# A state-space scan in chunks of 128 tokens with larger array tiles, ahead of routed experts

## The chip, the cores and the metric

The kernel runs on one core of one Trainium2 chip. The core has a matrix engine, TensorE (PE in the rows, with its weight loads as PEld), VectorE (DVE), ScalarE (ACT), GpSimd (POOL) and SyncE (SP, used here to issue DMAs). The metric is the device time of one execution in microseconds (us). All data are 32-bit floats except where the routing uses small whole numbers in bf16. In a profile's rows a 32-bit product appears as two weight loads and two matmuls (MATMUL, MM below); a transpose by the identity appears as one of each.

## The reference

Two stages. The first is a gated linear scan for 4 batches of 8 heads, 768 tokens, head size 32 and state size 16:

```python
for c in range(nc):                        # chunk = 32 tokens
    cum = np.cumsum(log_a[chunk], axis=-1)
    M = (Cc @ Bc.T) * exp(cum_i - cum_j) * causal
    y[chunk] = M @ xc + (Cc @ state) * exp(cum)
    state = exp(cum[-1]) * state + sum_j(Bc_j * xc_j * exp(cum[-1] - cum_j))
```

The size of the chunk is free: any one gives the same y. The second stage takes the 3072 tokens, 256 wide (8 heads side by side), finds for each the expert (of 8) with the largest cosine, and computes

```python
out[mask] = gate_w[mask, None] * (np.maximum(x[mask] @ w1[e], 0.0) @ w2[e])   # 256 -> 1024 -> 256
```

## The kernel before, in words

**Units.** A unit is 128 tokens of one batch, so there are 24, taken in pairs p = 0 to 11; chunk c (128 tokens of all 4 batches) holds the pairs 2c and 2c+1. Decays are divided out beforehand: `scale_b` scales B by the inverse decay (DVE), `scale_c` spreads the decay over partitions with a product by a 0/1 matrix (L251) and multiplies C by it (`cp`, DVE). The 8 heads of a unit lie in four groups q of 32 partitions, two heads (v = 0, 1) to a group with 16 states each.

**The products of a pair.** The scan itself runs in half chunks of 64 tokens (h = 0, 1), on small tiles of the PE array. `inner` (L312): 32 products of B and C, one for each head and half, on tiles of 32 rows by 64 columns, 64 columns moving. `outputs` (L340): 32 products of the carried state with C, on tiles of 32 by 32; and (L351) 32 products of the masked B-C products `g` with x, on tiles of 64 by 32. `sums` (L266): 16 products of B and x that give a chunk's contribution to the state. `finish` (L371): 4 products that turn the output back into rows of tokens and add the logits. `turn_b` (L233): 2 transposes. L251: 2 products. Together 120 products and transposes. `split_b` makes two copies of B, each with the other head of a group set to zero by `tmask` (ACT). `states` carries the state from half chunk to half chunk (DVE) and leaves it in `T`.

**The order.** `mamba` is a software pipeline: turn i of its loop does `inner` of pair i, `outputs` of pair i-1, `finish` of pair i-2, and the preparations of pair i+2. PE runs this in the order in which it is written (`manual_schedule`); the other engines' queues are ordered by a scheduler. In every odd turn from 5 on, `place` (L532) finds with bf16 products where the tokens of an earlier chunk go, and POOL sends them to the experts' lists in DRAM by four indirect DMAs (L546); `pick` prepares that on DVE. `load` and `load_weights` issue the DMAs of inputs and experts' weights from SP.

**After the scan** (`moe`), the experts' lists are read back (`xg`), transposed, and run through two layers of 128x128 products with 416 tokens moving (L635, L649), expert by expert. The change does not touch this part.

PSUM has 8 banks: `pg` takes four, `py` two, `pz` two.

Of the kernel before, what the change touches and what calls it, by code (L numbers as in the profile page):

```python
# [46 lines left out]
def build_consts(k):  # L47
# [15 lines left out]
    nc.vector.memset(k.heads[:, 0:Q:SQ], 1.0)  # L63
# [7 lines left out]
    k.mask = k.mc.tile([128, HQ], F32, name="mask")  # L71
    nc.gpsimd.memset(k.mask[:], 1.0)
    for h in range(2):
        m = k.mask[HQ * h : HQ * h + HQ]
        nc.gpsimd.affine_select(
            out=m, in_=m, pattern=[[1, HQ]], compare_op=ALU.is_ge, fill=0.0, base=0, channel_multiplier=-1
        )
# [23 lines left out]
def decays(k, kk):  # L101

    nc = k.nc
    tt = nc.vector.tensor_tensor
    a, f, r = k.a0[:, kk, :], k.f[:, kk, :], k.r[:, kk, :]
    clip(k, a)
    at = k.mc.tile([128, 4], F32, name=f"at{kk}")
    nc.vector.tensor_copy(out=at[:], in_=a[:, 0:Q:SQ])
    nc.vector.memset(a[:, 0:Q:SQ], 0.0)
    nc.vector.tensor_tensor_scan(out=f, data0=a, data1=k.heads[:], initial=0.0, op0=ALU.mult, op1=ALU.add)  # L110
    w = k.mc.tile([128, 2, 2], F32, name=f"w{kk}")
    tt(out=w[:, 0, :], in0=f[:, SQ - 1 : Q : HQ], in1=at[:, 1:4:2], op=ALU.mult)
# [15 lines left out]
def between(k):  # L128

    nc = k.nc  # L130
    a = k.a1
    clip(k, a[:])
    at = k.mc.tile([NB * NH, NK], F32, name="at")
    nc.vector.tensor_copy(out=at[:], in_=a[:, SQ:S:HQ])
    nc.vector.memset(a[:, SQ:S:HQ], 0.0)
    one = k.mc.tile([NB * NH, S], F32, name="one")
    nc.vector.memset(one[:], 0.0)
    nc.vector.memset(one[:, SQ:S:HQ], 1.0)
    p = k.mc.tile([NB * NH, S], F32, name="p")
    nc.vector.tensor_tensor_scan(out=p[:], data0=a[:], data1=one[:], initial=0.0, op0=ALU.mult, op1=ALU.add)  # L140
    k.g = k.mc.tile([NB * NH, NK - 1], F32, name="g")
    nc.vector.tensor_tensor(out=k.g[:], in0=p[:, HQ + SQ - 1 : S : HQ], in1=at[:, 1:], op=ALU.mult)


def spread_between(k):

    nc = k.nc
    ps = k.pz[:, 1, 448 : 448 + NB * (NK - 1)]
    for b in range(NB):
        nc.tensor.matmul(  # L150
            ps[:, (NK - 1) * b : (NK - 1) * (b + 1)], lhsT=k.spread[0:32, b, :], rhs=k.g[:], start=True, stop=True
        )
    k.whole = k.mc.tile([128, NK - 1, NB, 2], F32, name="whole")
    for v in range(2):
        nc.vector.tensor_scalar(
            out=k.whole[:, :, :, v], in0=ps.rearrange("p (b k) -> p k b", b=NB), scalar1=k.tmask[:, v : v + 1],
            scalar2=None, op0=ALU.mult,
        )
# [31 lines left out]
def load(k, c):  # L190
# [7 lines left out]
    t.st = k.inp.tile([128, 2, NB, 64], F32, name="st", tag="st", bufs=2)  # L198
# [37 lines left out]
def split_b(k, p):  # L236

    s = k.un[p] = Net()
    s.bt = k.work.tile([128, 2, 2, Q], F32, name="bt", tag="bt", bufs=3)
    for v in range(2):  # L240
        k.nc.scalar.activation(s.bt[:, v], k.pz[:, :, 264:392], ACT.Copy, scale=k.tmask[:, v : v + 1])


def scale_c(k, p):
# [5 lines left out]
    for i in range(2):  # L250
        nc.tensor.matmul(  # L251
            k.py[:, i, 384:512], lhsT=k.spread[g : g + 32, b + i, :], rhs=k.f[g : g + 32, c // 4, :],
            start=True, stop=True, tile_position=(g, 0),
        )
    s.cp = k.work.tile([128, 2, Q], F32, name="cp", tag="cp", bufs=4)
    nc.vector.tensor_tensor(out=s.cp[:], in0=t.ct[:, b : b + 2, :], in1=k.py[:, :, 384:512], op=ALU.mult)


def sums(k, p):

    c, b, t = pair(k, p)
# [12 lines left out]
def keep_sums(k, p):
    c, b, t = pair(k, p)
    k.nc.scalar.copy(  # L276
        out=t.st[:, :, b : b + 2, :], in_=k.py[:, :, 256:384].rearrange("p h (b m) -> p h b m", b=2)
    )


def states(k, c):


    nc = k.nc
    st = k.ld[c].st
    for h in range(2):
        i = 2 * c + h
        if i > 0:
            k.T[i] = k.stp.tile([128, NB, 2, D], F32, name="T", tag="T", bufs=6)
            nc.vector.tensor_tensor(  # L290
                out=k.T[i][:], in0=k.V[:].rearrange("p b (t d) -> p b t d", t=2),
                in1=k.whole[:, i - 1].unsqueeze(3).to_broadcast([128, NB, 2, D]), op=ALU.mult,
            )
        if i == 0:
            nc.vector.tensor_copy(out=k.V[:], in_=st[:, h])
        elif i < NK - 1:
            nc.vector.tensor_tensor(
                out=k.V[:], in0=k.T[i][:].rearrange("p b t d -> p b (t d)"), in1=st[:, h], op=ALU.add
            )


def inner(k, p):

    nc = k.nc
    s = k.un[p]
    for i in range(2):
        for v in range(2):
            for q in range(4):
                for h in range(2):
                    r, m = slice(32 * q, 32 * q + 32), slice(HQ * h, HQ * h + HQ)  # L310
                    a = 128 * i + HQ * v
                    nc.tensor.matmul(  # L312
                        k.pg[m, q, a : a + HQ], lhsT=s.bt[r, v, i, m], rhs=s.cp[r, i, m], start=True, stop=True,
                        tile_position=(32 * q, HQ * h),
                    )
    s.g = k.work.tile([128, 4, 4, HQ], F32, name="g", tag="g", bufs=2)
    nc.vector.tensor_tensor(  # L317
        out=s.g[:], in0=k.pg[:, :, 0:256].rearrange("p q (t i) -> p q t i", t=4),
        in1=k.mask[:].unsqueeze(1).unsqueeze(1).to_broadcast([128, 4, 4, HQ]), op=ALU.mult,
    )  # L320


def outputs(k, p):

    nc = k.nc
    c, b, t = pair(k, p)
    s = k.un[p]

    def at(i, q, h, v):
        a = 128 * i + HQ * v  # L330
        return k.py[32 * q : 32 * q + 32, h, a : a + HQ]

    for i in range(2):
        for v in range(2):
            for h in range(2):
                if 2 * c + h == 0:
                    continue
                for q in range(4):
                    r = slice(32 * q, 32 * q + 32)
                    nc.tensor.matmul(  # L340
                        at(i, q, h, v), lhsT=k.T[2 * c + h][r, b + i, v, :], rhs=s.cp[r, i, HQ * h : HQ * h + HQ],
                        start=(i == 0 and v == 0), stop=False, tile_position=(32 * q, 32 * q),
                        skip_group_check=True,
                    )
    for i in range(2):
        for v in range(2):
            for q in range(4):
                for h in range(2):
                    r = slice(HQ * h, HQ * h + HQ)
                    n = 32 * (4 * v + q)  # L350
                    nc.tensor.matmul(  # L351
                        at(i, q, h, v), lhsT=t.x[r, b + i, n : n + 32], rhs=s.g[r, q, 2 * i + v, :],
                        start=(2 * c + h == 0 and i == 0 and v == 0), stop=True, tile_position=(HQ * h, 32 * q),
                        skip_group_check=True,
                    )


def keep_outputs(k, p):
    s = k.un[p]
    s.yT = k.work.tile([128, 2 * KD, 2, HQ], F32, name="yT", tag="yT")  # L360
    k.nc.scalar.copy(  # L361
        out=s.yT[:].rearrange("p j h s -> p h j s"), in_=k.py[:, :, 0:256].rearrange("p h (j s) -> p h j s", j=4)
    )


def finish(k, p):

    yT = k.un[p].yT
    for i in range(2):
        for j, at in ((0, 0), (1, LG)):  # L370
            k.nc.tensor.matmul(  # L371
                k.pz[:, i, at : at + Y1], lhsT=yT[:, 2 * i + j].rearrange("p h s -> p (h s)"), rhs=k.turn[:, j, :],
# [9 lines left out]
def mamba(k):  # L382
# [15 lines left out]
    for i in range(-2, NP + 2):  # L398
# [28 lines left out]
        if i + 2 < NP:  # L427
            split_b(k, i + 2)
# [456 lines left out]
```

## Time and profile before

| | us |
|---|---|
| three runs | 361.54, 363.76, 366.12 |
| median | 363.76 |
| the profiled execution: its own time | 364.13 |
| the profiled execution: its span | 362.4 |
| PE busy / DVE / ACT / POOL | 290.1 / 116.8 / 65.2 / 73.8 |

Busy time is the time in which an engine has an instruction under way. A PE that has several small tiles at work counts once, and a PE that is busy need not be at its peak. "Idle <- issue" means that the engine waited for nothing that the profile can name. The row PEclk tells the clock that TensorE was granted, in tenths, as far as the trace recorded a change of it.

### The profile page before, as it was taken

Reading aid. Unit: us, or ns where it says so; the run is one execution under the profiler, and the core shown is the slowest. Engines: PE = TensorE matmul, PEld = TensorE weight load, DVE = VectorE, ACT = ScalarE, POOL = GpSimd, SP = SyncE. Lnnn points to the kernel's source line nnn. Section 1 sums busy time; section 2 is a strip of 40 time slices with the busy share of each in tenths; the row PEclk is TensorE's granted clock in tenths of the full one; section 3 lists DMA queues with packets and bytes.
Section 4 is the critical chain, followed back from the end, with each engine's and each line's share of the span. In section 5 each row is a group of like instructions: output and inputs, shape, how many; then the busy total and the mean of one; then the engine's idle time right before and its main releaser. Section 6 shows DMA issues by size and latency. Waiting matters only on the chain.

```text
span 362.4 us, 8035 instructions
## 1 busy us (share of the span) xinstructions
PE 290.1 (80%) x3495; PEld 183.1 (51%) x3495; DVE 116.8 (32%) x365; ACT 65.2 (18%) x177; POOL 73.8 (20%) x88
## 2 busy tenths in 40 slices
PE   0176996676959580299999999999999999999950
PEld 0065785464838370255555555555555555555520
DVE  8633453051423116152142251421422404203020
ACT  2021332030212120151311212113112101111000
POOL 8200000404040407120140231311402303104031
PEclk9999999697695876579999999999999999999995
DMA  6999412101010102413144324442443100001000
GB/s 223 341 375 379 139 54 73 63 4 65 4 63 4 62 5 94 131 50 138 46 145 166 116 48 159 137 155 58 137 166 117 45 0 20 20 2 46 0 25 25
DMA packets 17885, 35.32 MB, mean 97 GB/s; under 512 B 2054, under 2 KB 10451, under 8 KB 17848
## 3 DMA queue, kind: packets, MB, share of 16 engines
q1 hardware_dynamic: 14168, 26.74, 22.3%
q0 software_dynamic: 2688, 6.50, 5.7%
q10 hardware_dynamic: 992, 1.55, 1.2%
q8 instruction: 28, 0.46, 0.5%
q14 instruction: 9, 0.07, 0.1%
HBM read 26.89 MB, written 8.14 MB: 97 GB/s over the span
## 4 chain that ended last, share of the span: by engine, by line
PE 60%; issue 18%; DMA 10%; DVE 3%; POOL 3%; ACT 2%; ACTq 1%; POOLq 0%; DVEq 0%; SPq 0%
PE hp L635 18%; PE yp L649 15%; DMA out_dram<-yo,to 7%; PE py L351 6%; PE pz L371 5%; PE py L340 4%; PE pg L312 3%; PE py L251 3%; PE py L266 2%; PE xt L626 1%; PE ot L663 1%; POOL rows L546 1%; POOL out_dram L666 1%; DMA xg<-rows 1%; DMA b<-in_B_dram 1%
## 5 line engine op out<-in xcount | busy, mean ns | idle before, releaser
L635 PE MATMUL hp<-xT,w 128*128 128x416 f32 x256 | 97.8, 523 | 0.0
L649 PE MATMUL yp<-hT,w 128*128 128x416 f32 x256 | 90.8, 513 | 0.0
L649 PEld LDWEIGHTS yp<-hT,w 128*128 128x128 f32 x256 | 48.1, 190 | 38.5 <-issue 38.5
L635 PEld LDWEIGHTS hp<-xT,w 128*128 128x128 f32 x256 | 47.4, 194 | 33.1 <-issue 31.7
L666 POOL DMA_INDIRECT out_dram<-yo,to x32 | 32.3, 1008 | 89.5 <-DVE yo L665 83.4
L546 POOL DMA_INDIRECT rows<-yt,row_of x24 | 23.4, 976 | 111.4 <-DVE row_of L544 66.4
L351 PE MATMUL py<-g,x 64*32 64x64 f32 x768 | 21.1, 267 | 16.0 <-issue 16.0
L641 DVE TENSOR_SCALAR hT<-hp 128x416 f32<-128x416 f32 x32 | 18.9, 592 | 41.6 <-PE hp L635 28.5
L639 ACT ACTIVATE hT<-hp 128x416 f32<-128x416 f32 x32 | 16.6, 518 | 83.0 <-PE hp L635 60.2
L351 PEld LDWEIGHTS py<-g,x 64*32 64x32 f32 x768 | 12.9, 127 | 24.1 <-issue 23.5
L605 POOL TENSOR_TENSOR gr<-gr,half 104x4 f32<-104x4 f32 x8 | 8.3, 1037 | 78.4 <-ACT sq L601 78.4
L361 ACT COPY yT<-py 128x512 f32<-128x512 f32 x12 | 7.0, 586 | 69.8 <-PE py L266 55.5
L371 PE MATMUL pz<-turn,yT 128*128 128x136 f32 x96 | 19.2, 359 | 0.4 <-DVE oh L540 0.4
L665 DVE TENSOR_SCALAR yo<-ot,gate 104x256 f32<-104x256 f32 x32 | 15.4, 480 | 11.5 <-PE ot L663 11.5
L626 PE MATMUL xt<-ident,xg 104*128 104x104 f32 x64 | 7.8, 269 | 13.5 <-DMA xg<-rows 13.5
L371 PEld LDWEIGHTS pz<-turn,yT 128*128 128x128 f32 x96 | 16.2, 248 | 1.8 <-issue 0.8
L601 ACT ACTIVATE sq<-xg 104x256 f32<-104x256 f32 x32 | 12.9, 404 | 20.1 <-DMA xg<-rows 20.1
L656 DVE COPY yoT<-yp 128x416 f32<-128x416 f32 x8 | 4.7, 591 | 36.2 <-PE yp L649 25.5
L340 PE MATMUL py<-cp,T 32*32 32x64 f32 x704 | 15.7, 246 | 0.3 <-issue 0.3
L317 DVE TENSOR_TENSOR g<-pg,mask 128x1024 f32<-128x1024 f32 x12 | 14.7, 1222 | 2.9 <-PE pg L312 2.9
L251 PE MATMUL py<-f,spread 32*128 32x128 f32 x48 | 11.7, 380 | 4.8 <-ACT st L276 4.7
L663 PEld LDWEIGHTS ot<-ident,yoT 128*104 128x104 f32 x64 | 6.9, 129 | 16.6 <-DVE yo L665 9.6
(142 smaller groups left out, 224.4 us busy)
## 6 DMA issues: line engine op xcount, KB each, us to landing
w<-in_moe_w_dram SPq DMA_DIRECT2D x16, 1024.0 KB
xg<-rows SPq DMA_DIRECT2D x8, 442.0 KB
x<-in_x_dram SPq DMA_DIRECT2D x6, 512.0 KB
b<-in_B_dram SPq DMA_DIRECT2D x6, 256.0 KB
ct<-in_CT_dram SPq DMA_DIRECT2D x6, 256.0 KB
rows<-none ACTq DMA_DIRECT2D x8, 170.0 KB
out_dram<-yo,to POOLq DMA_INDIRECT x32
rows<-yt,row_of POOLq DMA_INDIRECT x24
```

The source lines that it names most:

```text
L251: nc.tensor.matmul(k.py[:, i, 384:512], lhsT=k.spread[g : g + 32, b + i, :], rhs=k.f[g : g + 32, c // 4, :], start=True, stop=True, tile_p ...
L317: nc.vector.tensor_tensor(out=s.g[:], in0=k.pg[:, :, 0:256].rearrange("p q (t i) -> p q t i", t=4), in1=k.mask[:].unsqueeze(1).unsqueeze(1 ...
L340: nc.tensor.matmul(at(i, q, h, v), lhsT=k.T[2 * c + h][r, b + i, v, :], rhs=s.cp[r, i, HQ * h : HQ * h + HQ], start=(i == 0 and v == 0), s ...
L351: nc.tensor.matmul(at(i, q, h, v), lhsT=t.x[r, b + i, n : n + 32], rhs=s.g[r, q, 2 * i + v, :], start=(2 * c + h == 0 and i == 0 and v == ...
L371: k.nc.tensor.matmul(k.pz[:, i, at : at + Y1], lhsT=yT[:, 2 * i + j].rearrange("p h s -> p (h s)"), rhs=k.turn[:, j, :], start=(j == 0), s ...
L546: d = nc.gpsimd.indirect_dma_start(out=k.rows[:, :], out_offset=bass.IndirectOffsetOnAxis(ap=row[:, b : b + 1], axis=0), in_=k.yt[:, NB * ...
L635: nc.tensor.matmul(t[:], lhsT=s.w1[:, j, 128 * f : 128 * f + 128], rhs=s.xT[:, j, :], start=(j == 0), stop=(j == KD - 1))
L639: nc.scalar.activation(s.hT[:, f, :], t[:], ACT.Relu)
L641: nc.vector.tensor_scalar_max(s.hT[:, f, :], t[:], 0.0)
L649: nc.tensor.matmul(t[:], lhsT=s.w2[:, f, 128 * j : 128 * j + 128], rhs=s.hT[:, f, :], start=(f == 0), stop=(f == KF - 1),)
L665: nc.vector.tensor_scalar_mul(y[:], t[:tr, :], s.gate[:, i : i + 1])
L666: d = nc.gpsimd.indirect_dma_start(out=k.out[:, :], out_offset=bass.IndirectOffsetOnAxis(ap=s.to[:, i : i + 1], axis=0), in_=y[:], in_offs ...
```

## The change

The scan runs in chunks of 128 tokens instead of 64, with larger tiles of the array:

- `inner`: per unit four products, one for each group q, on tiles of 32 rows by 128 columns, 256 columns moving (both heads of a group side by side). Now C is split by heads (`cm`, two ACT operations, from SBUF) and B is one plain copy (`keep_b`, one ACT operation). The four banks of `pg` are filled twice as far, and DVE applies the mask in two operations of 128x1024 instead of one.
- the state's part (`outputs_before`): per unit two products on the whole array. Their weights are `T`, in which each head's state stands in its own block and the rest is zero; POOL writes it, four operations of 128x256 per chunk.
- `outputs_within`: 16 products per pair, 128 rows by 32 columns, 128 columns moving. `sums`: 8 products per pair, 128 rows by 32 columns; they stay in PSUM, where `states` reads them (the ACT copy `keep_sums` is gone).
- `py` takes one bank, and a new bank `pf` holds the sums and the spread decays. In a turn, `finish` and `turn_b` stand ahead of the outputs.
- Decays are normalised at the middle of 128 tokens instead of 64.

```diff
 def scale_c(k, p):
...
+    s.cm = k.work.tile([128, 2, 2, Q], F32, name="cm", tag="cm", bufs=3)
+    for v in range(2):
+        nc.scalar.activation(s.cm[:, :, v, :], s.cp[:], ACT.Copy, scale=k.tmask[:, v : v + 1])
...
+def states(k, c):
+    nc = k.nc
+    st = k.pf[:, 0:256].rearrange("p (b m) -> p b m", b=NB)
+    if c == 0:
+        nc.vector.tensor_copy(out=k.V[:], in_=st)
+    else:
+        nc.vector.tensor_tensor(
+            out=k.V[:], in0=k.V[:], in1=k.whole[:, :, c - 1 : c].to_broadcast([128, NB, 64]), op=ALU.mult
+        )
+        nc.vector.tensor_tensor(out=k.V[:], in0=k.V[:], in1=st, op=ALU.add)
+    for b in range(NB):
+        T = k.stp.tile([128, 2, 4, D], F32, name="T", tag="T", bufs=8)
+        k.T[NB * (c + 1) + b] = T
+        nc.gpsimd.tensor_tensor(
...
+            op=ALU.mult,
+        )
+
+def inner(k, p):
...
     for i in range(2):
+        for q in range(4):
+            r = slice(32 * q, 32 * q + 32)
+            nc.tensor.matmul(
+                k.pg[:, q, 256 * i : 256 * i + 256], lhsT=s.bt[r, i, :], rhs=s.cm[r, i], start=True, stop=True,
+                tile_position=(32 * q, 0),
+            )
...
+def outputs_before(k, p):
...
+    for i in range(2):
+        T = k.T.pop(2 * p + i)
+        for v in range(2):
+            k.nc.tensor.matmul(
+                k.py[:, 2 * i + v, :], lhsT=T[:, v].rearrange("p q d -> p (q d)"), rhs=s.cp[:, i, :],
+                start=(i == 0 and v == 0), stop=False, skip_group_check=True,
             )
...
+def outputs_within(k, p):
...
     for i in range(2):
         for v in range(2):
             for q in range(4):
+                n = 32 * (4 * v + q)
+                k.nc.tensor.matmul(
+                    k.py[32 * q : 32 * q + 32, 2 * i + v, :], lhsT=t.x[:, b + i, n : n + 32], rhs=s.g[i][:, q, v, :],
+                    start=(c == 0 and i == 0 and v == 0), stop=True, tile_position=(0, 32 * q),
+                    skip_group_check=True,
+                )
```

PE's row of instructions for one turn in the middle of the scan before the change, turn 7 (`pg`, `py`, `pz` are the PSUM tiles; "x32" counts the products that stand in a row):

```order
L312 MATMUL pg<-cp,bt 64x64 x32
L340 MATMUL py<-cp,T 32x64 x32
L351 MATMUL py<-g,x 32x64 x32
L266 MATMUL py<-x,bp 32x64 x16
L371 MATMUL pz<-turn,yT 128x136 x4
L233 MATMUL pz<-ident,bp 128x128 x2
L251 MATMUL py<-f,spread 128x128 x2
```

The same turn on PE in the changed program (L308 `inner`, L362 `finish`, L236 `turn_b`, L330 and L344 the outputs, L270 `sums`, L252 the spread of the decays):

```order
L308 MATMUL pg<-cm,bt 128x256 x8
L362 MATMUL pz<-turn,yT 128x136 x4
L236 MATMUL pz<-ident,bp 128x128 x2
L330 MATMUL py<-cp,T 128x128 x4
L270 MATMUL pf<-x,bp 32x64 x8
L344 MATMUL py<-g,x 32x128 x16
L252 MATMUL pf<-f,spread 128x128 x2
```

The products of the state and of `g` moved behind `finish` and `turn_b`, and 120 became 44.

POOL's queue around the first two sets of indirect DMAs in the changed program (before the change the 24 indirect DMAs L546 stood there with nothing between them; L291 is the multiplication that writes `T`, L537 the indirect DMA):

```order
L291 TENSOR_TENSOR T_536<-V_171,blocks_279 128x256
L291 TENSOR_TENSOR T_538<-V_171,blocks_279 128x256
L291 TENSOR_TENSOR T_540<-V_171,blocks_279 128x256
L291 TENSOR_TENSOR T_542<-V_171,blocks_279 128x256
L537 DMA rows_57<-yt_128,row_of_640 24576x272 x4
L291 TENSOR_TENSOR T_699<-V_171,blocks_279 128x256
L291 TENSOR_TENSOR T_701<-V_171,blocks_279 128x256
L291 TENSOR_TENSOR T_703<-V_171,blocks_279 128x256
L291 TENSOR_TENSOR T_705<-V_171,blocks_279 128x256
L537 DMA rows_57<-yt_128,row_of_798 24576x272 x4
```

Twenty multiplications were added to that queue, four for each of the chunks 1 to 5; the last eight stand between indirect DMAs.

## Rows read from the trace of the kernel before

**Rows 1.** The page: span, granted clock in 40 slices of 9.06 us.

```profile
span 362.4 us, 8035 instructions
...
PEclk9999999697695876579999999999999999999995
```

**Rows 2.** Chain of waits, pieces in order: start us, length us, what.

```profile
43.71 2.08 PE pz L371 x8
...
153.50 13.78 PE hp L635 x32
...
168.00 11.20 PE yp L649 x32
```

**Rows 3.** Windows (twelve turns; turns 1, 3, 5): PE, PEld, DVE, ACT, POOL, clock, DMA.

```profile
26.20:129.90 103.70, 79.83 (x2604) 64.09 (x2608) 33.96 (x85) 22.46 (x51) 15.63 (x16) 0.84 0.24 84
29.90:39.90 10.00, 6.28 (x205) 4.73 (x205) 3.50 (x7) 1.60 (x4) 0.00 (x0) 1.00 0.86 310
46.60:52.00 5.40, 5.17 (x244) 4.47 (x243) 2.63 (x5) 2.20 (x7) 0.00 (x0) 1.00 0.03 6
61.40:73.30 11.90, 9.09 (x244) 6.76 (x241) 2.96 (x7) 1.64 (x4) 4.10 (x4) 0.71 0.15 51
```

**Rows 4.** Timeline of PE in turn 3: start us, length us, line, shapes, count.

```profile
46.57 0.91 PE L312 MATMUL pg<-cp,bt 32*64 32x64 f32 x64
47.41 1.09 PE L340 MATMUL py<-cp,T 32*32 32x64 f32 x64
...
49.99 1.19 PE L371 MATMUL pz<-turn,yT 128*128 128x136 f32 x8
...
51.34 0.71 PE L251 MATMUL py<-f,spread 32*128 32x128 f32 x4
51.97 0.34 PE L312 MATMUL pg<-cp,bt 32*64 32x64 f32 x12
```

**Rows 5.** Timeline of PE in turn 8, behind a set of indirect DMAs.

```profile
93.02 1.28 PE L312 MATMUL pg<-cp,bt 32*64 32x64 f32 x64
94.23 1.93 PE L340 MATMUL py<-cp,T 32*32 32x64 f32 x64
```

**Rows 6.** PE's waits from 26.2 to 129.9: us in total, times, longest us.

```profile
PE py L351 <- issue: 16.0, 31, 2.8
...
PE pz L532 <- ACT bt L241: 2.4, 3, 0.8
```

**Rows 7.** Chain of waits, the three longest pieces of issue during the scan.

```profile
33.29 3.34 issue
...
54.74 2.81 issue
...
75.98 1.20 issue
```

**Rows 8.** Windows from the start into the first two of them, columns as Rows 3.

```profile
0.00:35.00 35.00, 14.55 (x349) 11.24 (x350) 19.42 (x67) 5.60 (x13) 9.80 (x24) 1.00 0.92 328
0.00:56.50 56.50, 31.77 (x989) 25.54 (x989) 29.44 (x91) 11.87 (x28) 9.80 (x24) 1.00 0.69 244
```

**Rows 9.** DMA queues from 26.2 to 129.9: packets, MB, share.

```profile
q8 instruction: 21, 0.34, 1.4%
```

**Rows 10.** Windows of L351 alone (PE, PEld): turn 3; first and last of four stretches.

```profile
46.60:52.00 5.40, 1.08 (x64) 0.76 (x64) 1.00 0.03 6
...
63.10:68.90 5.80, 2.83 (x47) 1.29 (x47) 0.76 0.26 91
...
121.30:127.00 5.70, 2.14 (x33) 0.94 (x36) 0.75 0.27 98
```

**Rows 11.** Groups by line: count | busy us, mean ns | idle before.

```profile
L317 DVE TENSOR_TENSOR g<-pg,mask 128x1024 f32<-128x1024 f32 x12 | 14.7, 1222 | 2.9 <-PE pg L312 2.9
...
L182 POOL COPY turn<-ident 128x128 f32<-128x128 f32 x1 | 1.8, 1836 | 0.0
...
L183 POOL COPY turn<-ident 128x128 f32<-128x128 f32 x1 | 0.3, 281 | 0.0
```

More of the change, by code (lines that the diff above doesn't have):

```diff
@@ L70, in build_consts @@
     )
-    k.mask = k.mc.tile([128, HQ], F32, name="mask")
-    nc.gpsimd.memset(k.mask[:], 1.0)
[L73 to L77, printed above, removed]
+    block = k.mc.tile([128, 4], F32, name="block")
+    nc.vector.memset(block[:], 0.0)
+    for q in range(4):
+        nc.vector.memset(block[32 * q : 32 * q + 32, q : q + 1], 1.0)
+    k.own = k.mc.tile([128, 2, 4], F32, name="own")
+    for v in range(2):
+        nc.vector.tensor_scalar_mul(k.own[:, v, :], block[:], k.tmask[:, v : v + 1])
+    k.mask = k.mc.tile([128, Q], F32, name="mask")
+    nc.gpsimd.memset(k.mask[:], 1.0)
+    nc.gpsimd.affine_select(
+        out=k.mask[:], in_=k.mask[:], pattern=[[1, Q]], compare_op=ALU.is_ge, fill=0.0, base=0,
+        channel_multiplier=-1,
+    )
     k.half = pool.tile([128, NU], F32, name="half")
@@ L233, in turn_b, with keep_b @@
         k.nc.tensor.transpose(k.pz[:, i, 264:392], t.bp[:, b + i, :], k.ident[:])
-def split_b(k, p):
+def keep_b(k, p):
     s = k.un[p] = Net()
-    s.bt = k.work.tile([128, 2, 2, Q], F32, name="bt", tag="bt", bufs=3)
-    for v in range(2):
-        k.nc.scalar.activation(s.bt[:, v], k.pz[:, :, 264:392], ACT.Copy, scale=k.tmask[:, v : v + 1])
+    s.bt = k.work.tile([128, 2, Q], F32, name="bt", tag="bt", bufs=3)
+    k.nc.scalar.copy(out=s.bt[:], in_=k.pz[:, :, 264:392])
 def scale_c(k, p):
@@ L274, in keep_sums @@
[L274 to L278, printed above, removed]
+    for i in range(b, b + 2):
+        for q in range(4):
+            k.nc.tensor.matmul(
+                k.pf[32 * q : 32 * q + 32, 64 * i : 64 * i + 64], lhsT=t.bp[:, i, 32 * q : 32 * q + 32],
+                rhs=t.x[:, i, :].rearrange("p (t q d) -> p q t d", t=2, q=4)[:, q],
+                start=True, stop=True, tile_position=(0, 32 * q),
+            )
@@ L281, in states @@
 def states(k, c):
     nc = k.nc
[L285 to L299, printed above, removed]
+    st = k.pf[:, 0:256].rearrange("p (b m) -> p b m", b=NB)
@@ L302, in inner @@
 def inner(k, p):
     nc = k.nc
+    s = k.un[p]
+    s.g = []
+    for i in range(2):
+        for q in range(4):
+            r = slice(32 * q, 32 * q + 32)
+            nc.tensor.matmul(
+                k.pg[:, q, 256 * i : 256 * i + 256], lhsT=s.bt[r, i, :], rhs=s.cm[r, i], start=True, stop=True,
+                tile_position=(32 * q, 0),
+            )
+    for i in range(2):
+        g = k.work.tile([128, 4, 2, Q], F32, name="g", tag="g", bufs=4)
+        nc.vector.tensor_tensor(
+            out=g[:], in0=k.pg[:, :, 256 * i : 256 * i + 256].rearrange("p q (t i) -> p q t i", t=2),
+            in1=k.mask[:].unsqueeze(1).unsqueeze(1).to_broadcast([128, 4, 2, Q]), op=ALU.mult,
+        )
+        s.g.append(g)
@@ L305, in inner @@
+def outputs_before(k, p):
+    c, b, t = pair(k, p)
+    s = k.un[p]
+    if c == 0:
+        return
+    for i in range(2):
+        T = k.T.pop(2 * p + i)
+        for v in range(2):
+            k.nc.tensor.matmul(
+                k.py[:, 2 * i + v, :], lhsT=T[:, v].rearrange("p q d -> p (q d)"), rhs=s.cp[:, i, :],
+                start=(i == 0 and v == 0), stop=False, skip_group_check=True,
+            )
+def outputs_within(k, p):
+    c, b, t = pair(k, p)
     s = k.un[p]
@@ L308, in inner @@
             for q in range(4):
[L309 to L320, printed above, removed]
@@ L323, in outputs @@
[L323 to L355, printed above, removed]
@@ L358, in keep_outputs @@
+                n = 32 * (4 * v + q)
+                k.nc.tensor.matmul(
+                    k.py[32 * q : 32 * q + 32, 2 * i + v, :], lhsT=t.x[:, b + i, n : n + 32], rhs=s.g[i][:, q, v, :],
+                    start=(c == 0 and i == 0 and v == 0), stop=True, tile_position=(0, 32 * q),
+                    skip_group_check=True,
+                )
 def keep_outputs(k, p):
     s = k.un[p]
[L360 to L363, printed above, removed]
+    s.yT = k.work.tile([128, 2 * KD, Q], F32, name="yT", tag="yT")
@@ L366, in finish @@
+    k.nc.scalar.copy(out=s.yT[:], in_=k.py[:])
 def finish(k, p):
@@ L371, in finish @@
             k.nc.tensor.matmul(
-                k.pz[:, i, at : at + Y1], lhsT=yT[:, 2 * i + j].rearrange("p h s -> p (h s)"), rhs=k.turn[:, j, :],
+                k.pz[:, i, at : at + Y1], lhsT=yT[:, 2 * i + j, :], rhs=k.turn[:, j, :],
                 start=(j == 0), stop=(j == 1), skip_group_check=True,
@@ L427, in mamba @@
         if i + 2 < NP:
-            split_b(k, i + 2)
+            keep_b(k, i + 2)
+        if 0 <= i - 1 < NP:
+            outputs_before(k, i - 1)
+        if i + 2 < NP and (i + 2) // 2 < NC - 1:
+            sums(k, i + 2)
+        if 0 <= i - 1 < NP:
+            outputs_within(k, i - 1)
+            keep_outputs(k, i - 1)
+        if i == -1:
+            spread_between(k)
+        if i % 2 and i + 2 < NP and (i + 2) // 2 < NC - 1:
+            states(k, (i + 2) // 2)
+        if i + 2 < NP:
             scale_c(k, i + 2)
@@ L828 @@
         k.pg = ps.tile([128, 4, 512], F32, name="pg")
-        k.py = ps.tile([128, 2, 512], F32, name="py")
+        k.py = ps.tile([128, 2 * KD, Q], F32, name="py")
+        k.pf = ps.tile([128, 512], F32, name="pf")
         k.pz = ps.tile([128, 2, 512], F32, name="pz")
```

89 lines of the change are left out of this document (35 added, 54 removed).

## The prediction, made before the changed kernel ran

> **What bounds the kernel now.** I read the page first, then the chain of waits, then the scan turn by turn in windows. The experts' part is PE streaming 416 columns at a time: 32 MMs in 11.20 us [rows 2], 350 ns each, 0.84 ns a column. Nothing in it is changed, so I leave its time alone. The scan's twelve turns take 103.7 us, from 26.2 to 129.9 [rows 3], on average 8.6. An undisturbed turn, turn 3, takes 5.4. So some 39 us of the scan are not work at full pace, and the question is which of that the change takes out. Three things make it up.
>
> First, code. PE stops for 3.34, 2.81 and 1.20 us with nothing to wait for that the profile can name [rows 7]. Up to the first stop it had begun 349 + 350 = 699 instructions, up to the second 1978 [rows 8]; the difference, 1279, is within one of 5 x 256. During the scan the instruction queue moved 21 packets, 0.34 MB together, about 16 KB each [rows 9]: 256 instructions of 64 bytes. I read these stops as PE at the end of a block of code whose successor has not arrived. A turn in the middle has 244 + 243 instructions on PE [rows 3], nearly two blocks in 5.4 us.
>
> Second, POOL's indirect DMAs. In a clean turn L351's 64 MMs are over in 1.08 us; in each of four stretches in which POOL issues a set of four they take about 5.7 us, in bursts, though nothing named holds them [rows 10]. In the first and last of these PE began 94 and 69 instructions in 11.5 us, 14 a microsecond. That is 4 x 4.6 = 18 us, and most of the 16.0 us of issue before L351 [rows 6].
>
> Third, the clock. Behind such a stretch turn 8 runs at the lower level, 1.2 GHz: L312 takes 1.21 us instead of 0.84, L340 1.86 instead of 1.03 [rows 4, 5]. The page has these dips in slices 8 to 16 [rows 1]. At 43.7 us L371 still takes 2.08 us, where turn 3 needs 1.35 for it and the transposes together [rows 2, 4], though the page shows 9 there. I therefore take the first 45 us as lower level too: the recorded clock begins only with its first change.
>
> **The change, part by part.** *PE's array time.* Rates at full clock: 0.84 ns a column and MM. `inner`: 16 MMs of 256 columns are 3.4 us in a row, 0.86 if the four row tiles work at once. L312's 64 MMs of 64 columns would be 3.4 us in a row too and take 0.84, so tiles do overlap; but L251, four MMs on one row tile, takes 0.63 us, 158 ns each, instead of 108 [rows 4], so 50 ns of weight load is not hidden on a row tile. Four MMs per tile give 1.06; I take 1.15. `finish` and `turn_b` stay at 1.35. `outputs_before`: 8 MMs of 128 columns on the whole array, 0.9. `sums`: 0.2 if the four column tiles overlap, 0.9 if not; I take 0.3. `outputs_within`: 32 MMs of 128 columns, 0.86 to 3.4; L340's 64 MMs, also 3.4 us in a row, need 1.03 on four tiles that share neither rows nor columns, and I take 1.0. Weight loads on whole columns of rows seem hidden: `finish` and the transposes stream 8 x 136 and 2 x 128 columns, 1.13 us, and take 1.35. A rule of the Trainium skill speaks against it (TensorE: Matmul & The Clock Gate, Part 3, The mechanism): a weight load overlaps a running MM only if it goes to another group of rows, and all tiles of `outputs_within` span all rows. With its P/1.2 ns for P columns that is, as an estimate, 32 x 27 ns or 0.9 us more a turn, and 360 us in the end. L252 0.63. Four changes between tile shapes 0.45. A turn: 5.8 us, against 5.4 now. By itself the new tiling is no gain.
>
> The first turns lack products (`finish` in turns 0 and 1, outputs in 0, the state's part in 0 to 2), the last ones the preparations: 12 x 5.8 - 9 = 60.6 us.
>
> *Code.* 42 products at four instructions and 2 transposes at two are 172 a turn, a block in 1.5 turns. A stop of PE lasted 3.34 us at most, and a block now lasts over 8. I count no stop: 7.4 us go, already out of the sum.
>
> *Indirect DMAs.* They are all still there, in the same odd turns, behind the same `place`. At 14 instructions a microsecond the 5.7 us hold 80. If they begin with `outputs_before`, these are 16, all 32 of `sums` and 32 of `outputs_within`, worth 1.7 us at full pace: a loss of 4.0. If they begin with `finish`, whose MMs hardly need more than that pace, the loss is 2.9. I take 3.6, four times: 14.4 us instead of 18. Ends: 0, if wider products are spared, and 4.6.
>
> *Clock.* Before, PE ran some 4 to 9 us at the lower level behind each such stretch. I keep that: 8.5 us in all, and 6 us for turns 0 to 2, the higher level coming somewhat earlier because the 3.34 us gap is gone.
>
> *Waits.* `place` waited for the copies of B (2.4 us in three turns [rows 6]); the copy now stands half a turn earlier, so nothing. DVE gets 1.22 us more a turn from the second mask operation [rows 11], and loses two state operations in a pair of turns: from 34.0 / 12 = 2.8 to about 4 us, under 5.8; ACT stays near 1.9 [rows 3]. `g` is needed a turn later, `pg` again after all of `finish` to L252, so both hide under PE; without that cover DVE would cost its 1.22 us a turn.
>
> *POOL* gets twenty multiplications of 256 elements. No row shows one. Bounds from copies of 128 elements: 2 x 0.28 and 2 x 1.84 us [rows 11]; I take 1 us, near the lower, because the two copies differ only in what else was running. The last two of four must wait on PE until the old `T` is read; behind them stand POOL's next indirect DMAs and, on DVE, the next update of V with `cp` and `g` behind it. Two multiplications then have the rest of a turn, over 2 us, before `cp` is due: nothing at 1 us; at 3.67 us a delay of some 2 us in three turns, 6 to 7 us.
>
> *Sum.* 60.6 + 14.4 + 8.5 + 6 = 89.5 us instead of 103.7; the approach and the tail, eight indirect DMAs in a row before the lists can be read, stay. 364.1 - 14.2 = 350 us. The profiled execution, 364.13, is 0.4 above the median of the runs.
>
> **The rivals.** (B) *The clock stays up.* PE's array is fuller in the new turns, since MMs last as long as the work and not as long as their issue, so the lower level may not follow a stretch. Against it: the stretches themselves remain. 350 - 8.5 = 341.
>
> (C) *Wide products are spared.* The slow stretches were seen with L351's narrow MMs alone. If they do not bite, 14.4 and 8.5 go: 327. For it: the experts' MMs show no such stops beside POOL's DMAs. Against it: those come at under 6 instructions a microsecond (two for each MM of 350 ns [rows 2]), which 14 allows.
>
> (D) *The stops are not code*, but something per product or per time. Then 7.4 us stay: 357. For it stands the Trainium skill (Runtime: NRT & Kernel Launch, section Instruction fetch mechanics), which says that code arrives in blocks of 16 KiB and that a crossing is mostly hidden. The trace agrees on the block and not on the hiding: two stops 1279 instructions apart.
>
> (E) *The other side: POOL's multiplications slow PE as its DMAs do.* PE then issues 14 a microsecond where a turn wants 30, and loses half of POOL's added time: at 3.67 us each 73 us of POOL, 37 of PE: 387. It decides from about 2.1 us each, where 350 + 21 is 371. Against it: while POOL is in the indirect DMAs it builds transfers; a multiplication has none, and the two copies ran before the scan, beside no dense PE work. Nothing in the trace excludes it.
>
> That the array's tiles work one after another (2.3 + 2.4 + 0.6 us more a turn) would give over 400, but L312 and L340 rule it out.
>
> **The numbers.** Chances: the forecast 0.45 (343 to 359), B 0.22, C 0.13, D 0.10, E and other losses 0.10. The likeliest is 350. The range goes from 326 (C, or B with a cheaper turn) to 361 (D with a turn dearer by 0.3 us); what lies outside is half of C and most of E. Two per cent, what a measurement here can tell, is 7.3 us: faster means under 356.5. That takes nearly nine tenths of the forecast, B, C and half of D: 0.79. Within: 0.14. Slower: 0.07, from E.
>
> **What would show it.** Turns 3 and 4 near 5.8 us with L308 near 1.15 and L344 near 1.0; no stop of over 1 us at a multiple of 256 instructions; `sums` and `outputs_within` stretched to 4 us and more in turns 5, 7, 9 and 11; the granted clock lower behind them. I am wrong on code if stops of that size remain, on the DMAs if L270 and L344 are not stretched, on POOL if PE waits for `T` or is stretched in turns 1 and 3, where POOL has multiplications and no DMAs.

## The result and the profile after

| | us |
|---|---|
| changed kernel, median of 4 (332.30 to 337.37) | 336.19 |
| kernel before, median of 4 (361.54 to 366.12) | 364.71 |
| ratio, 95% interval | 0.919 (0.908 to 0.930) |
| forecast | 350, range 326 to 361 |

The kernel became faster by 28.5 us, twice the 14 that were forecast. (The ratio is that of the means, 334.89 and 364.27 us, and leaves out the run of 337.37 us, whose granted clock was the lowest of the four.) The changed kernel's page: span, granted clock in slices of 8.36 us, and the instruction queue.

```profile
span 334.2 us, 4458 instructions
...
PEclk9999999799797757999999999999999999999985
...
q8 instruction: 14, 0.23, 0.3%
```

The span is 28.2 us shorter than in [rows 1]. Windows of the changed kernel, columns as in Rows 3: turn 3 (no indirect DMAs), turn 6 (behind the first set of four), and the twelve turns.

```profile
43.00:48.00 5.00, 5.00 (x94) 4.35 (x91) 4.18 (x9) 2.34 (x6) 0.74 (x2) 1.00 0.32 105
58.60:67.80 9.20, 8.64 (x96) 6.41 (x95) 4.25 (x11) 2.85 (x6) 3.49 (x6) 0.81 0.10 34
...
26.00:101.60 75.60, 68.41 (x912) 53.83 (x912) 45.01 (x91) 25.09 (x54) 27.32 (x35) 0.95 0.33 117
```

Against [rows 3] the scan fell from 103.7 to 75.6 us, 28.1 less: all of the gain lies there. Approach (26.2 and 26.0 us) and tail are as before. Turn 3 takes 5.00 us where 5.8 were forecast. Its timeline on PE (start us, length us, line, shapes, count):

```profile
43.96 1.19 PE L362 MATMUL pz<-turn,yT 128*128 128x136 f32 x8
44.99 0.38 PE L236 MATMUL pz<-ident,bp 128*128 128x128 f32 x2
45.20 1.06 PE L330 MATMUL py<-cp,T 128*128 128x128 f32 x8
46.19 0.43 PE L270 MATMUL pf<-x,bp 128*32 128x64 f32 x16
46.44 1.06 PE L344 MATMUL py<-g,x 128*32 128x128 f32 x32
47.43 0.37 PE L252 MATMUL pf<-f,spread 32*128 32x128 f32 x1
47.44 0.48 PE L308 MATMUL pg<-cm,bt 32*128 32x256 f32 x2
```

A row's start less that of the row above it is a step's price: `finish` with `turn_b` 1.24, `outputs_before` 0.99, `sums` 0.25, `outputs_within` 0.99, together 3.47. A change of tile shape is inside these prices: the trace's single MMs of `outputs_before` start 0.11 us apart, and the first of `sums` starts 0.205 us behind the last of them, so that the change costs some 0.09 us. L252 (tiles of one row group) runs among the first products of the next `inner`, which use all four; the two together take 1.50 us.

From turn 5 on two stretches of the twelve turns run at 1.2 GHz, and a third follows right behind the turns. Windows of the three; the lower level lasts 3.4 us in each:

```profile
60.95:64.45 3.50, 3.50 (x18) 2.75 (x19) 2.30 (x4) 1.39 (x3) 0.28 (x1) 0.51 0.01 2
88.25:91.75 3.50, 2.82 (x12) 2.82 (x13) 2.69 (x3) 1.99 (x4) 0.00 (x0) 0.51 0.02 5
101.95:105.40 3.45, 3.45 (x24) 3.21 (x26) 0.00 (x0) 0.60 (x1) 0.00 (x0) 0.51 0.02 5
```

Before there were four, 34.1 us together; one of the longer ones in the trace of the kernel before:

```profile
86.60:96.80 10.20, 9.37 (x267) 7.89 (x270) 4.08 (x12) 2.20 (x5) 0.50 (x1) 0.50 0.07 23
```

What a set of four indirect DMAs does now is not what it did before. In [rows 10] PE got L351 in small bursts. The last set of the changed kernel, first POOL, then PE, then ACT (the bracket is the idle time ahead of the row and what ended it):

```profile
95.15 0.96 POOL L537 DMA_INDIRECT rows<-yt,row_of  x1 [8.01 <-issue]
...
98.94 0.96 POOL L537 DMA_INDIRECT rows<-yt,row_of  x1 [0.30 <-issue]
```

```profile
95.71 1.05 PE L330 MATMUL py<-cp,T 128*128 128x128 f32 x8
96.69 1.08 PE L344 MATMUL py<-g,x 128*32 128x128 f32 x32
101.64 1.65 PE L362 MATMUL pz<-turn,yT 128*128 128x136 f32 x7 [3.87 <-ACT yT L354]
```

```profile
101.01 0.58 ACT L354 COPY yT<-py 128x512 f32<-128x512 f32 x1 [4.50 <-remote]
```

PE has `outputs_within` over at 97.77, at full pace. ACT's copy of it begins at 101.01, 1.1 us behind the end of POOL's fourth DMA (99.90), and the next `finish` waits for the copy ("remote" means that the profile found no instruction that released it). The trace's semaphore events show what is late: the signal that the last MM of `outputs_within` gives is recorded at 100.93. So this set costs PE's consumers a late start rather than PE its pace.

All four sets of turns 5 to 11 show the late start. The copy begins at 61.04, 75.83, 88.29 and 101.01, 1.0 to 1.2 us behind the end of the fourth DMA each time, and the signal comes 2.7 to 3.2 us behind the end of its MM; in the run with the DMAs behind the scan (below) none of PE's signals in the twelve turns comes more than 0.2 us late. In the first two sets PE loses pace as well, mostly in the next turn's `inner`. Turns 5 and 6:

```profile
56.81 1.41 PE L344 MATMUL py<-g,x 128*32 128x128 f32 x32
...
60.06 0.37 PE L308 MATMUL pg<-cm,bt 32*128 32x256 f32 x1 [0.17 <-issue]
60.79 1.85 PE L308 MATMUL pg<-cm,bt 32*128 32x256 f32 x10 [0.36 <-issue]
62.58 2.09 PE L362 MATMUL pz<-turn,yT 128*128 128x136 f32 x8
```

The 16 MMs of L308 take 4.0 us here, from 58.59 to 62.58, where turn 5 needs 1.1; the last 1.5 us of that are at the lower level.

### The profile page after: what moved, and what is told of

It reads as the page before. It is cut to its first block, busy times and chain, and to the rows that moved or that the text cites. A ratio compares the mean times of both kernels' runs of the same rounds, so it can differ in the third digit from the quotient of the medians.

```text
span 334.2 us, 4458 instructions
## 1 busy us (share of the span) xinstructions
PE 278.9 (83%) x1687; PEld 173.4 (52%) x1687; DVE 125.7 (38%) x371; ACT 66.6 (20%) x177; POOL 86.0 (26%) x107
## 4 chain that ended last, share of the span: by engine, by line
PE 59%; issue 20%; DMA 11%; DVE 5%; POOL 1%; ACTq 1%; ACT 1%; POOLq 0%; SPq 0%; DVEq 0%
PE hp L626 19%; PE yp L640 17%; DMA out_dram<-yo,to 8%; PE pg L308 6%; PE pz L362 4%; PE py L344 2%; PE py L330 2%; PE pf L252 2%; DMA rows<-none 2%; PE xt L617 2%; PE ot L654 1%; PE pf L270 1%; POOL out_dram L657 1%; DMA xg<-rows 1%; DVE g L314 1%
## 5 line engine op out<-in xcount | busy, mean ns | idle before, releaser
L537 POOL DMA_INDIRECT rows<-yt,row_of x24 | 23.4, 976 | 30.5 <-issue 21.1
L314 DVE TENSOR_TENSOR g<-pg,mask 128x1024 f32<-128x1024 f32 x24 | 28.2, 1219 | 6.5 <-PE pg L308 6.5
L291 POOL TENSOR_TENSOR T<-V,blocks 128x256 f32<-128x256 f32 x20 | 12.6, 653 | 41.0 <-DVE blocks L159 14.6
L308 PE MATMUL pg<-cm,bt 32*128 32x256 f32 x192 | 21.8, 479 | 1.2 <-issue 0.9
L362 PE MATMUL pz<-turn,yT 128*128 128x136 f32 x96 | 17.5, 336 | 5.9 <-ACT yT L354 5.9
L362 PEld LDWEIGHTS pz<-turn,yT 128*128 128x128 f32 x96 | 14.8, 229 | 10.2 <-ACT yT L354 7.0
L656 DVE TENSOR_SCALAR yo<-ot,gate 104x256 f32<-104x256 f32 x32 | 15.4, 480 | 11.5 <-PE ot L654 11.5
L308 PEld LDWEIGHTS pg<-cm,bt 32*128 32x128 f32 x192 | 13.3, 220 | 4.4 <-issue 3.8
L645 ACT COPY yoT<-yp 128x416 f32<-128x416 f32 x8 | 4.1, 506 | 56.9 <-PE yp L640 56.9
L584 DVE TENSOR_REDUCE gm<-xg 104x4 f32<-104x32 f32 x8 | 1.5, 182 | 37.0 <-DMA xg<-rows 37.0
```

The source lines that it names most:

```text
L308: nc.tensor.matmul(k.pg[:, q, 256 * i : 256 * i + 256], lhsT=s.bt[r, i, :], rhs=s.cm[r, i], start=True, stop=True, tile_position=(32 * q, 0),)
L314: nc.vector.tensor_tensor(out=g[:], in0=k.pg[:, :, 256 * i : 256 * i + 256].rearrange("p q (t i) -> p q t i", t=2), in1=k.mask[:].unsqueez ...
L362: k.nc.tensor.matmul(k.pz[:, i, at : at + Y1], lhsT=yT[:, 2 * i + j, :], rhs=k.turn[:, j, :], start=(j == 0), stop=(j == 1), skip_group_ch ...
L537: d = nc.gpsimd.indirect_dma_start(out=k.rows[:, :], out_offset=bass.IndirectOffsetOnAxis(ap=row[:, b : b + 1], axis=0), in_=k.yt[:, NB * ...
L656: nc.vector.tensor_scalar_mul(y[:], t[:tr, :], s.gate[:, i : i + 1])
```

## The experiments

The theory to test: (1) the smaller number of instructions takes away stops for code; (2) larger tiles themselves cost the same array time; (3) what is left, 75.6 us against twelve turns of 5, is the indirect DMAs and the clock behind them. Rivals: it is the order of the turn; it is any transfer beside PE; it is written bytes.

Two measures below: "twelve turns", from turn 0's first MM to turn 12's; and "turns 5 to 11", the part of it in which the four sets of indirect DMAs of turns 5, 7, 9 and 11 stand.

| kernel | time | twelve turns | turns 5 to 11 |
|---|---|---|---|
| changed, first profile | 335.96 | 75.6 | 48.4 |
| changed, again | 334.7 (4 runs) | 76.5 | 51.0 |
| indirect DMAs behind the scan | 343.94 | 60.2 | 34.7 |
| plain DMAs instead, SP / POOL | 343.7 / 343.56 | 60.2 / 60.3 | 34.7 / 34.7 |
| 4-byte indirect DMAs instead | 356.58 | 71.0 | 45.4 |
| a split that the scheduler undid | 332.02 | 72.0 | 46.5 |
| fills on POOL | 327.54 | 73.5 | 47.9 |
| fills on POOL, sets of 3 + 1 | 319.48 | 64.7 | 39.2 |
| fills on POOL, sets of 2 + 2 | 311.85 | 60.2 | 34.7 |
| the same, again | 315.06 (4 runs) | 63.6 | 36.3 |
| fills on POOL, 1 + 1 + 1 + 1 | 314.04 | 60.2 | 34.7 |

**Indirect DMAs behind the scan.** In `place`, kept for later:

```diff
-    row = w.tile([128, NB], I32, name="row_of", tag="row_of")
-    nc.vector.tensor_copy(out=row[:], in_=m[:])
-    for b in range(NB):
-        d = nc.gpsimd.indirect_dma_start(...)
+    nc.vector.tensor_copy(out=k.mall[:, c, :], in_=m[:])
```

and all 24 issued behind the last `place`. The same edit in the kernel before.

> The changed kernel with its 24 indirect DMAs all issued behind the scan instead of in turns 5 to 13. Theory (POOL's indirect DMAs hold PE up while POOL issues them): the twelve turns take 60 to 63 us instead of 75.6, no turn of 5 to 11 is over 5.6 us and the clock does not fall in the scan; the whole is some 5 us slower all the same, about 341 us, since 24 DMAs of 1.27 us now stand in a row behind the scan instead of 8. Rival (the long turns have another cause, such as a wait of the new turn itself): the turns stay at 75 us and the whole goes to 355.

> The kernel before with its 24 indirect DMAs all issued behind the scan. Theory: the twelve turns take 72 to 77 us instead of 103.7: 18 us of stretched products and some 11 us of lower clock go, the three stops at ends of code blocks (7.4 us) stay; the whole is about 355 us. Against the changed kernel treated the same way the difference of the scan is then 12 to 15 us, what code and the early clock make. Rival: the turns stay above 95 us.

The changed kernel took 343.94 us, its twelve turns 60.2, at full clock and with no stop of PE of over 0.45 us where a block of code ends:

```profile
26.21:86.40 60.19, 58.92 (x912) 48.36 (x912) 45.28 (x91) 25.52 (x54) 12.09 (x19) 1.00 0.30 108
```

(The end is later because all 24 DMAs now stand ahead of the experts' lists.) The kernel before took 366.23 us instead of about 355; its twelve turns were expected at 72 to 77 and took 82.0. What explains the miss is its chain of waits (start us, length us):

```profile
33.99 3.07 issue
...
54.92 2.26 issue
...
64.80 1.16 issue
...
71.80 1.34 issue
...
79.60 1.53 issue
...
86.67 1.65 issue
...
95.46 0.85 issue
```

By PE's instructions in order (the few of its sequencer counted in) the stops in which PE is idle for over 0.45 us without a wait that the profile names stand at numbers 705, 1985, 2497, 3009, 3521, 4033, 4545, 4801 and 5313: all of the form 705 + 256 n. From one instruction's start to the next they last 0.72 to 3.38 us each, together 15.6 us. The DMA records of the same trace tell what ends them: each ends 1.2 to 1.6 us behind the end of a 16 KB packet of the instruction queue. Most lie 512 instructions and 7 to 9 us apart; from 54.8 to 104.6 us that queue's packets start 3.8 us apart on average, 3.4 at the least. An undisturbed turn (243 + 244 instructions in 5.4 us [rows 3]) goes through 512 in 5.7, a block in 2.8: PE would be faster than its code.

So the difference between the two kernels without DMAs in the scan, 82.0 - 60.2 = 21.8 us, is 15.6 of code and 6.2 of the rest. That is (1), shown, and it is larger than it looked in the trace of before. As to (2), the array time did not grow: an undisturbed turn takes 5.0 us instead of 5.4. Of the 28.1 us that the scan gained, 21.8 are there without any DMAs in it; the other 6.3 are that the sets cost 103.7 - 82.0 = 21.7 us before and 75.6 - 60.2 = 15.4 now. The trace of before, with the sets, shows fewer stops for code. I explain that so (it was not tried by itself): the slow L351 in each set of DMAs gave the next block time to arrive.

**Plain DMAs at the same places**, 128 rows of the same bytes to a scratch in DRAM, the indirect ones behind the scan; once from SP's queue and once from POOL's:

```diff
+        for b in range(NB):
+            nc.gpsimd.dma_start(k.spare[c * NB + b], k.yt[:, NB * c + b, :])
```

> The changed kernel with its indirect DMAs behind the scan and, in turns 5 to 13 where they stood, plain DMAs of the same bytes issued by SP into a spare place in DRAM (twenty of 139 KB; the real ones follow). Theory (what holds PE up is POOL at work on the DMAs, not the bytes): turns as in the run without any, 60 to 63 us. Rival (the transfers are what holds PE up): turns as in the changed kernel, 73 to 77 us.

> As the run with plain DMAs from SP, but issued from POOL's queue, which also makes its transfers in software. Theory: PE is held up as by indirect ones wherever POOL shows a span of about 1 us for each, so the turns take 70 to 77 us; if a plain DMA costs POOL much less, proportionally less. Rival (it is the indirection): 60 to 63 us.

Twelve turns of 60.2 and 60.3 us: nothing lost, although POOL was in the four of them for 2.44 us:

```profile
53.29 2.44 POOL L556 DMA_DIRECT2D spare<-yt  x4 [2.87 <-DVE yt L554]
```

So it is not the transfer, from either queue. Whether it is the indirection, this run does not tell: the four plain DMAs keep POOL for 2.44 us, about as long as two indirect ones (2.37 us in the kernel with sets of two below), and those cost nothing either. A row of plain DMAs as long as four indirect ones was not tried.

**Indirect DMAs of 4 bytes a row** at the places, the real ones late (`in_=k.yt[:, NB * c + b, TOK : TOK + 1]`).

> The changed kernel (fills on ACT's queue as in it) with the 24 indirect DMAs behind the scan and, at their places in the turns, 20 indirect DMAs of one element in a row (4 bytes instead of 1088) to a scratch in DRAM. Work added, none left out. If the written rows hold up PE, the turns take 60 to 62 us as with all DMAs late and the time is 343 to 346. If it is the issue of an indirect DMA on POOL, whatever it carries, the turns take 73 to 77 us and the time is 357 to 362.

356.58 us, twelve turns 71.0, between the two expectations and nearer to the second: most of the loss (10.8 of 15.4 us) is there without the bytes. A detail does not fit the simple form: the first set cost nothing. Turns 5, 7 and 9 of this run:

```profile
51.00:55.56 4.56, 4.56 (x88) 3.89 (x84) 4.04 (x11) 1.78 (x4) 2.73 (x3) 1.00 0.37 119
61.39:68.14 6.75, 6.35 (x90) 4.64 (x87) 4.00 (x12) 1.97 (x5) 3.88 (x4) 1.00 0.01 0
75.54:83.39 7.85, 7.85 (x68) 6.58 (x68) 4.63 (x13) 2.26 (x5) 3.88 (x4) 0.57 0.01 0
```

Why is open.

**The turn's order alone**, in the kernel before: `finish` and `turn_b` ahead of the outputs, 120 products as before.

> The kernel before with the turn's order of the changed one alone (the token products and the B turns ahead of the outputs, products still 120 in a pair). If the gain is the smaller number of instructions, the turns stay within 3 us of 103.7 and the time at 360 to 367 us. If the order does it, turns of 5.0 to 6 us as in the changed kernel show where no code stop is, and the time goes below 350.

366.7 us, its twelve turns 103.3 (from 29.7 to 133.0): the order by itself is not the gain.

**Splitting a set in the program's order.** Two of the four stand behind a second conversion of row numbers, written a turn later.

> The changed kernel, but of the four indirect DMAs of each place in turns 5, 7, 9 and 11 two are issued at once and two a turn later. If the hold on PE comes from four of them queued in a row (PE runs on, but what it reports arrives late, until the fourth is through), two in a row are covered by the slack that yT and cp have, the turns cost 60 to 64 us instead of 75.6, the clock keeps its level, and the time is 321 to 326 us. If each indirect DMA costs PE its share wherever it stands, the turns stay at 73 to 77 us and the time at 334 to 338; if the cost is one for each set of calls, eight sets make it longer still, 80 us and above.

332.02 us, at the lower end of what the changed kernel itself takes; it tells nothing of the theory. POOL's rows show four DMAs in a row as ever, because VectorE's queue is ordered by the scheduler, which put the two conversions side by side:

```profile
53.03 1.22 POOL L520 DMA_INDIRECT rows<-yt,row_of  x1 [2.86 <-ACT cm L262]
...
57.09 0.96 POOL L520 DMA_INDIRECT rows<-yt,row_of  x1 [0.30 <-DVE bp L220]
```

**Fills on POOL's queue.** ScalarE stands 7.8 us issuing the eight fills of the lists, ahead of the first C scaling. The changed kernel (ACTq is ACT's DMA issue):

```profile
13.31 0.37 ACT L242 COPY bt<-pz 128x256 f32<-128x256 f32 x1 [4.92 <-PE pz L236]
13.37 7.83 ACTq L483 DMA_DIRECT2D rows<-none  x8
21.25 0.91 ACT L262 ACTIVATE cm<-cp,tmask 128x256 f32<-128x256 f32 x2 [7.58 <-DMA rows<-none]
```

```diff
-        nc.scalar.dma_start(
+        nc.gpsimd.dma_start(
```

> The changed kernel with the eight fill transfers of the rows buffer issued from POOL's queue instead of ACT's, where ACT stands 7 us (13.4 to 21.3) before the scan's first turns. If ACT's stand is what the approach waits for, turn 0 starts 4 to 6 us earlier (20 to 22 instead of 26.0) and the time is 330 to 332 us. If the approach waits for the loads anyway, which share the DMA engines with the fills, it starts at 25 to 26 and the time is 335 to 337.

> Both edits together, the split places and the fills on POOL's queue. If both theories hold, 316 to 322 us; if only the split does, 321 to 326; if neither, 334 to 338. Beside it the kernel before is timed again: 361 to 366 us as before, or near 342, if what the last look gave (342.2) is one of its ordinary times.

The fills alone: 327.54 us, less than expected, with turn 0 at 19.49 instead of 26.0. With the split that was none: 327.72 (five runs), the same. The scaling now starts at 15.75:

```profile
15.75 0.91 ACT L262 ACTIVATE cm<-cp,tmask 128x256 f32<-128x256 f32 x2
```

**Splitting a set by data.** The later row numbers are added to zero times a value that comes late, so no scheduler can move them:

```diff
+        nc.vector.scalar_tensor_tensor(
+            out=row[:], in0=late, scalar=0.0, in1=m[:, at:to], op0=ALU.mult, op1=ALU.add
+        )
...
+        if i % 2 == 1 and 5 <= i < 5 + 2 * (NC - 2):
+            issue(k, *k.later, 2, 4, k.un[i - 1].yT[:, 0, 0:2])
```

> The changed kernel with the fills on POOL's queue, and of each place's four indirect DMAs (turns 5, 7, 9, 11) two behind the yT copy of that turn: their row numbers are added to zero times a value of yT, so that no order of VectorE can move them forward. (In after_split the two conversions of row numbers had been moved together, and the four DMAs stood in a row as before.) If a row of four is what costs, the turns fall from 75 us to 62 to 66, and the time from 327.6 to 315 to 320 us. If each indirect DMA costs its share wherever it stands, the time stays at 325 to 330.

> The same with one indirect DMA at a time: one at once, one behind yT of that turn, one behind the token rows of the next, one behind yT of the next. If the hold lasts as long as DMAs stand queued in a row, each is covered and the time is 313 to 318 us; if each costs its share (15 us over 16 DMAs, near 0.95 each), 325 to 330.

> As after_gate2 (fills on POOL's queue), but three of the four indirect DMAs at once and one behind that turn's yT. If the hold begins with the third in a row, the turns lose 1 to 2 us at each of the four places beside after_gate2's 60 us, and the time is 315 to 321 us. If it begins only with the fourth, or only where POOL stands in DMAs longer than yT's slack, 311 to 314.

Two and two: 311.85 us, better than expected. POOL's rows of the first place, the second pair released by the row numbers:

```profile
46.71 1.09 POOL L522 DMA_INDIRECT rows<-yt,row_of  x1 [2.81 <-ACT cm L262]
48.11 0.98 POOL L522 DMA_INDIRECT rows<-yt,row_of  x1 [0.30 <-issue]
51.75 1.01 POOL L522 DMA_INDIRECT rows<-yt,row_of  x1 [0.73 <-DVE row_of L518]
53.06 0.97 POOL L522 DMA_INDIRECT rows<-yt,row_of  x1 [0.30 <-PE py L330]
```

All the same DMAs, and twelve turns of 60.2 us, turns 5 to 11 of 34.66: to the hundredth what the kernel without them took, and none of PE's signals in the turns is more than 0.2 us late. Turn 5 with two in a row, and (second fence) with three:

```profile
45.02:49.58 4.56, 4.56 (x88) 3.89 (x84) 3.97 (x10) 1.78 (x4) 2.25 (x3) 1.00 0.45 149
```

```profile
45.02:50.96 5.94, 5.51 (x89) 4.24 (x86) 3.96 (x10) 1.78 (x4) 3.04 (x3) 1.00 0.41 142
```

In the second, `outputs_within` stops at 49.87, 0.5 us behind the start of the third DMA (49.39), which it does not with two:

```profile
48.58 1.29 PE L344 MATMUL py<-g,x 128*32 128x128 f32 x27
50.18 0.43 PE L344 MATMUL py<-g,x 128*32 128x128 f32 x5 [0.31 <-issue]
```

A place thus costs the scan (turns 5 to 11, less 34.66, by four, the clock behind it included): 3.0 to 4.1 us with four in a row, 1.1 with three, 0 to 0.4 with two. The kernel meant to issue one at a time lost nothing either, though its last two ran into the first of the next place:

```profile
54.58 1.05 POOL L526 DMA_INDIRECT rows<-yt,row_of  x1 [0.30 <-DVE row_of L522]
...
57.34 0.97 POOL L526 DMA_INDIRECT rows<-yt,row_of  x1 [0.30 <-issue]
```

These three stand beside `inner` and `finish` of a turn that begins at 55.43 and are over before its `outputs_within` (58.99); in the kernel with 3 + 1 the third stood beside it. So I take it that not the number alone decides, but also which part of the turn the row reaches; no run moves one row through the turn to show it. It is no faster in the end (314.04): its last DMAs end 0.6 us later, and the rest of the 2.2 us is no more than single runs of one kernel differ by.

**The best version** (fills on POOL, two and two) and both kernels of the case once more on one chip:

> after_gate2 again, the version that the experiments point to, in rounds: 310 to 314 us, 0.85 to 0.86 of the kernel before.

> The changed kernel, unchanged, on the same chip as best: 332 to 337 us, as its first rounds gave.

> The kernel before, unchanged, with a profile on this chip. If the 342.2 us of one look was its other ordinary time, it shows here with fewer or shorter stops for code, or with the clock up from earlier on; otherwise 361 to 367 us.

The best: 315.06 us (314.39 to 316.11), 0.865 of the kernel before (0.860 to 0.870); the changed kernel 334.7, 0.920 (0.914 to 0.925); the kernel before 364.2. The best took 3 us more than the single run above: in its profile turns 0 to 4 last 27.3 instead of 25.5 us, with L308 at 2.09 us still in turn 2, and pairs of DMAs cost 0.4 us. The run of the kernel before at 342.2 us, once, did not come again (all others 361.5 to 367.1); no trace of it was kept, and it stays unexplained; against it the changed kernel would be only 2% faster.

## Why the prediction was right in sign and wrong in size

- *Code: right.* Stops at 705 + 256 n are shown, and in the changed kernel there is none of that size. Rival D falls. The Trainium skill (Runtime: NRT & Kernel Launch, Instruction fetch mechanics) says that a crossing is mostly hidden: hidden it is at 172 instructions in a turn of 5 us, and not where PE would take 256 in 2.8 us, with stops of up to 3.4 us.
- *A turn of 5.8 us, twelve turns of 60.6, and 6 for the clock of turns 0 to 2: 66.6 forecast.* Without DMAs and with the profile's own slower turns 0 to 4 (1.7 us; its recorded clock begins at 40.6 us, that of the run without DMAs at 35.7) it is 60.2 + 1.7 = 61.9. The term was 4.7 too dear. A turn in the middle is 5.0: `finish` to `outputs_within` take 3.47 us, changes of tile shape included, instead of 3.55 and 0.45 for the changes, and `inner` with L252 1.50 instead of 1.78. The lower level did rule turns 0 to 2, as forecast: L308 takes 2.17, 2.09 and 2.09 us there. How the 4.7 us divide between the turn and that clock, no row tells. By the Trainium skill's rule on weight loads (TensorE: Matmul & The Clock Gate, Part 3, The mechanism) `outputs_within` would have cost, as an estimate, 0.9 us more; its 32 MMs on full columns of rows took 0.99 us, weight loads included, so they are hidden.
- *Indirect DMAs 14.4 and clock 8.5: 22.9 forecast.* Measured: turns 5 to 11, 48.4 - 34.7 = 13.7. Here the forecast failed most, by 9.2 us. The larger part of that is the clock's term: 8.5 us were kept from before, and turns 5 to 11 hold two stretches of 3.4 us at the lower level, which cost at most half their length, 3.4 us. (In the second profile of the changed kernel the stretches are 13.7 us, at most 6.8 of cost.) That leaves at least 10.3 us for the hold, not far from 14.4, but this is luck, for the mechanism failed. The forecast let 14 instructions a microsecond hold PE in `sums` and `outputs_within` through 5.7 us, and gave L270 and L344 unstretched as the sign of being wrong. L270 keeps its 0.43 us beside the sets, and L344 takes 1.1 to 1.7 us instead of 4. What comes late is PE's signal to those that wait for it, by 2.7 to 3.2 us, and behind the first two sets the next `inner`; part of a set passes before anything is due. Rivals B (341) and C (327) each came half true, and 336 lies in the range only because it was drawn to hold both; the forecast's own 343 to 359 was missed.
- The two errors, 4.7 and 9.2, are the 13.9 us between 89.5 and 75.6.
- *POOL: right.* The multiplication took 653 ns, less than the 1 us taken:

```profile
L291 POOL TENSOR_TENSOR T<-V,blocks 128x256 f32<-128x256 f32 x20 | 12.6, 653 | 41.0 <-DVE blocks L159 14.6
```

  Turns 1 and 3, where it runs beside PE with no DMA, were not stretched, and the kernel with late DMAs keeps the same multiplications at 60.2 us. Rival E falls.
- *Waits: right.* DVE's second mask operation (1219 ns each) is covered in a turn of 5 us, in which DVE is busy 4.18; there is little more room.

What is shown is where the time goes, by taking it away. What in a row of indirect DMAs delays PE's signals is not. The transfer of the bytes is ruled out, and so is a DMA issued from POOL's queue as long as the row takes 2.4 us; rows of two, three and four cost different amounts. Open are a longer row of plain DMAs, the place in the turn by itself, and whether the recording of the trace has a share in it.

## What to carry to other kernels

Count PE's instructions against the block of 256: where a block is used up in less time than one arrives (3.8 us here), a change that only merges small products gains, even at the same array time, and a slow neighbour in the trace may be hiding how much. Look at how many indirect DMAs stand in a row beside dense products, and break the row up by a data dependency, since an order in the program text may be undone by the scheduler. And look at which engine issues a few large fills: here its other work stood 7.8 us behind them.

## What the runs showed of the hardware that was not expected

- Code for PE came at 3.8 us on average for a block of 256 instructions, with stops of 0.72 to 3.38 us where PE would have been faster.
- Three or four indirect DMAs in a row on POOL cost the scan 1.1 to 4.1 us a set where they reach the outputs; two 0 to 0.4; four plain DMAs on the same queue, which take POOL no longer than two indirect ones, nothing. Beside four in a row the signal of PE's last product of the outputs came 2.7 to 3.2 us late in the first profile.
- A change of tile shape cost some 0.09 us in the clean turn.
- ScalarE stood 7.8 us in eight DMA issues; POOL's queue took the same eight at no cost to the scan (73.5 us instead of 75.6).
